# Storing the four tail tiles of the output with one DMA per batch instead of one DMA per two batches

## The chip, the cores and the metric

The kernel runs on one core of one Trainium2 chip. The metric is the device time of one execution in microseconds (us). Three runs of the kernel before gave 993.57, 993.82 and 994.36 us, a median of 993.82 us.

## What is computed

Three layers follow each other, all in 32-bit floats. The last one is the one that the change touches: its result is what is stored.

```
attention: 8 batches, 8 heads, 576 tokens, head size 64, mask by blocks of 64 tokens
x   = attention output, as 4608 tokens (8 batches x 576) x 512
soft mixture of experts, 8 experts x 4 slots:
    logits    = x @ phi                          # 4608 x 32
    slot_in   = softmax over tokens(logits).T @ x
    slot_out  = per expert: relu(slot_in @ w1) @ w2
    y         = softmax over slots(logits) @ slot_out
feed-forward:
    out = relu(y @ w_in)**2 @ w_out              # 4608 x 512, float32
```

The output has 4608 rows of 512 floats (2 KB a row). The rows of one batch stand together: batch b holds rows 576 b to 576 b + 575.

## The kernel before

The 4608 tokens are handled as 36 tiles of 128 tokens. A batch has 576 tokens, which is four whole tiles (NU = 4) and a tail of 64. Tiles 0 to 31 are the whole tiles of the eight batches. Tiles 32 to 35 are tail tiles: each holds the 64 tail tokens of two neighbouring batches, the first batch on partitions 0 to 63 and the second on partitions 64 to 127.

The attention and the experts come first. The last stage is `ffn()`. It works through six groups of six tiles (NG = 6), and in each group through 16 blocks of the hidden width. In every block and for every tile, three matmuls (L1289, L1290, L1291) add to that tile's accumulator `po`, which fills one PSUM bank. Hidden blocks for later steps (`hidden`, L1237) are made two steps ahead.

In the last of a group's 16 blocks each tile is finished in turn, and `emit_out` is called right behind its third matmul. It does two things:

- L1260 copies `po` into an SBUF tile `ot` of 128 partitions x 512 floats. VectorE (DVE) copies the even tiles and ScalarE (ACT) the odd ones. There are six `ot` buffers.
- A DMA on SyncE's queue (SP) stores `ot` to the output. For tiles 0 to 31 this is L1263, 128 consecutive rows of the output. For tiles 32 to 35 this is L1266: the output is viewed as batches x tokens x width, and the DMA's destination is two batches x 64 tokens x 512.

The sixth group holds tiles 30 to 35, so the four tail tiles are the last four things that the kernel computes and stores. Nothing follows but the end of the program, where SP waits for the DMAs that are still under way (line L1350 in the profile) and the engines meet. The instructions of each engine keep the order that the program has; SP issues one DMA after another and does no arithmetic.

Of the kernel before, what the change touches and what calls it, by code (L numbers as in the profile page):

```python
# [23 lines left out]
def tile_attn_soft_moe_ffn(  # L24
# [12 lines left out]
    nc = tc.nc  # L37
    B, H, S, D = q.shape
# [7 lines left out]
    NU = S // 128  # L46
# [1134 lines left out]
    def ffn():  # L1181
# [76 lines left out]
        def emit_out(i, po):  # L1258
            ot = o_p.tile([128, DM], F32, tag="ot", name="ot")
            (nc.scalar.copy if i % 2 else nc.vector.tensor_copy)(ot, po)  # L1260
            if i < NU * B:
                r0 = S * (i // NU) + 128 * (i % NU)
                nc.sync.dma_start(out=out[r0:r0 + 128, :], in_=ot)  # L1263
            else:
                b0 = 2 * (i - NU * B)
                nc.sync.dma_start(out=out.rearrange("(b s) d -> b s d", s=S)[b0:b0 + 2, 128 * NU:S, :], in_=ot)  # L1266

        seq = [(g, f) for g in range(NTILE // NG) for f in range(KF)]
        hid = {}
# [9 lines left out]
        for i, (g, f) in enumerate(seq):  # L1279
# [7 lines left out]
            for t in range(NG):  # L1287
                sl = slice(128 * t, 128 * t + 128)
                nc.tensor.matmul(pos[t], gh[:, sl], woh[f], start=(f == 0), stop=False)  # L1289
                nc.tensor.matmul(pos[t], gh[:, sl], wol[f], start=False, stop=False)  # L1290
                nc.tensor.matmul(pos[t], gl[:, sl], woh[f], start=False, stop=(f == KF - 1))  # L1291
                if f == KF - 1:
                    emit_out(NG * g + t, pos[t])
# [61 lines left out]
```

## Time and profile before

| | |
|---|---|
| median of three runs | 993.82 us (993.57 to 994.36) |
| the profiled execution: its time | 995.41 us |
| the profiled execution: its span, first to last instruction | 993.6 us |
| TensorE (PE) busy | 906.1 us, 91% of the span |
| DVE, ACT, POOL busy | 601.0, 519.7, 261.8 us |
| DMA from the core | 113.02 MB, 47.5% of 16 engines' span on SP's queue |
| stores of the output | 36 DMAs of 256 KB |

The span runs from the first to the last instruction; 1.8 us of the profiled execution's time lie around it. A median of the runs stands 1.6 us below the profiled execution. The page cuts the span into 40 slices of 24.8 us. In its last slice PE's digit is 0 while the slice before is at 9.

### The profile page before, as it was taken

The numbers are of one execution on the slowest core, as the hardware profiler recorded it, in microseconds if no ns is written. First come the engines' busy times: TensorE is split into PE (matmuls) and PEld (weight loads), VectorE is DVE, ScalarE is ACT, GpSimd is POOL, SyncE is SP. The second block draws the span as 40 slices with busy tenths as digits, with TensorE's granted clock in tenths as the row PEclk, the third lists the DMA queues.
The fourth block names the chain that finished last, engine by engine and source line by source line (L and its number), as shares of the span: only waits on it lengthen the run. The fifth ranks groups of instructions, "written<-read, shape, count | busy, mean of one in ns | idle before, by whom it ended". The sixth has DMA issues, their size and how long they took to land.

```text
span 993.6 us, 19542 instructions
## 1 busy us (share of the span) xinstructions
PE 906.1 (91%) x7712; PEld 656.4 (66%) x7712; DVE 601.0 (60%) x1348; ACT 519.7 (52%) x916; POOL 261.8 (26%) x390
## 2 busy tenths in 40 slices
PE   3799999989899989998898989999999999999990
PEld 2456656666566646666345868888888888888880
DVE  6767688887779878654525795444435445444430
ACT  5678577767677666543125766344334334334320
POOL 0446546463655546462000340000000000000000
PEclk9989999999999999998897999999999999999996
DMA  7777887978678886678995221001001001001001
GB/s 149 159 158 157 130 178 157 185 157 160 141 162 172 177 177 130 156 209 280 325 276 196 85 85 64 1 1 64 1 1 64 1 1 64 1 1 64 1 0 63
DMA packets 233508, 113.02 MB, mean 114 GB/s; under 512 B 193992, under 2 KB 210376, under 8 KB 233416
## 3 DMA queue, kind: packets, MB, share of 16 engines
q1 hardware_dynamic: 233416, 111.78, 47.5%
q8 instruction: 60, 0.98, 0.4%
q14 instruction: 32, 0.26, 0.1%
HBM read 78.71 MB, written 9.44 MB: 89 GB/s over the span
## 4 chain that ended last, share of the span: by engine, by line
PE 60%; DVE 13%; DMA 10%; ACT 5%; SPq 4%; POOL 3%; issue 2%; DVEq 0%; ACTq 0%; POOLq 0%
PE po L1289 12%; PE po L1291 12%; PE po L1290 12%; PE xm L557 4%; PE ps_h L1237 3%; PE ps_sc L484 3%; DVE pm L421 3%; DMA t<-qb 3%; PE ps_h L1075 2%; DVE dec_sq L172 1%; POOL ul L667 1%; POOL ss L527 1%; DMA s<-ka 1%; PE ps_u L658 1%; DMA ar_lo<-in_q_dram 1%
## 5 line engine op out<-in xcount | busy, mean ns | idle before, releaser
L1290 PE MATMUL po<-wol,gh 128*128 128x512 f32 x576 | 224.5, 390 | 1.3 <-POOL wol L1221 1.3
L1291 PE MATMUL po<-woh,gl 128*128 128x512 f32 x576 | 224.9, 391 | 0.0
L1289 PE MATMUL po<-woh,gh 128*128 128x512 f32 x576 | 224.7, 392 | 0.0
L1247 ACT ACTIVATE r<-ps_h 128x768 f32<-128x768 f32 (+1 forms) x97 | 77.9, 804 | 207.3 <-PE ps_h L1237 207.3
L1254 DVE TENSOR_TENSOR sq<-r 128x768 f32<-128x768 f32 x80 | 76.7, 958 | 172.5 <-ACT r L1247 172.5
L522 ACT ACTIVATE p<-ps_sc,es 128x512 f32<-128x512 f32 x192 | 130.2, 687 | 78.6 <-PE ps_sc L493 63.0
L527 POOL TENSOR_TENSOR ss<-p 128x384 f32<-128x384 f32 (+1 forms) x128 | 93.2, 748 | 152.2 <-ACT p L522 152.1
L421 DVE TENSOR_REDUCE pm<-ps_max 128x4 f32<-128x512 f32 x160 | 108.0, 683 | 31.4 <-PE ps_max L415 31.3
L1291 PEld LDWEIGHTS po<-woh,gl 128*128 128x128 f32 x576 | 108.3, 188 | 24.1
L1289 PEld LDWEIGHTS po<-woh,gh 128*128 128x128 f32 x576 | 108.2, 188 | 23.7 <-ACT woh L1220 0.2
L1290 PEld LDWEIGHTS po<-wol,gh 128*128 128x128 f32 x576 | 108.5, 188 | 21.6 <-POOL wol L1221 1.8
L527 POOL TENSOR_TENSOR ss<-ss,p 128x320 f32<-128x320 f32 (+1 forms) x128 | 102.4, 800 | 51.2 <-ACT p L522 46.2
L484 PE MATMUL ps_sc<-t,s 128*128 128x512 f16 (+3 forms) x512 | 108.0, 306 | 7.5 <-ACT t L395 3.1
L1255 DVE TENSOR_TENSOR gl<-sq,gh 128x768 fp32r<-128x768 f32 (+1 forms) x97 | 93.0, 959 | 16.7 <-ACT sq L1252 6.7
L557 PE MATMUL xm<-p,ar_hi 128*64 128x256 f32 (+3 forms) x512 | 93.0, 455 | 0.0
L1248 ACT ACTIVATE gh<-r 128x768 fp32r<-128x768 f32 (+1 forms) x97 | 81.6, 841 | 2.8
L407 PE MATMUL ps_max<-s,t 128*128 128x128 f16 (+3 forms) x256 | 61.9, 307 | 4.2 <-DVE pm L421 3.7
L568 PEld LDWEIGHTS tl<-p,ar_hi 128*64 128x64 f32 x512 | 36.4, 140 | 36.5 <-issue 31.8
L493 PEld LDWEIGHTS <-s 128*128 128x128 f16 x512 | 45.6, 101 | 16.9 <-issue 6.7
L493 PE MATMUL ps_sc<-t,s 128*128 128x64 f16 x512 | 54.6, 195 | 0.0
L1237 PE MATMUL ps_h<-cts,ws 128*128 128x512 f32 x192 | 50.5, 343 | 2.7 <-ACT r L1247 2.3
L395 ACT COPY t<-ps_qT 128x1024 f16<-128x1024 f16 x64 | 40.4, 637 | 10.3 <-PE ps_qT L391 9.4
(210 smaller groups left out, 1362.0 us busy)
## 6 DMA issues: line engine op xcount, KB each, us to landing
wch<-in_moe_w_dram SPq DMA_DIRECT2D x12, 1024.0 KB, 8.2
out_dram<-ot SPq DMA_DIRECT2D x36, 256.0 KB, 2.1
ar_hi<-in_v_dram SPq DMA_DIRECT2D x64, 128.0 KB, 3.2
raw<-in_moe_w_in_dram SPq DMA_DIRECT2D x16, 512.0 KB, 5.4
wch<-in_moe_w_dram SPq DMA_DIRECT2D x32, 256.0 KB, 6.0
ar_hi<-in_moe_w_dram SPq DMA_DIRECT2D x6, 1024.0 KB, 8.9
s<-s SPq DMA_DIRECT2D x32, 144.0 KB, 2.7
ar_lo<-in_k_dram SPq DMA_DIRECT2D x32, 128.0 KB, 3.2
```

What stands on the lines that cost most here:

```text
L421: nc.vector.tensor_reduce(out=o, in_=i, axis=AX.X, op=ALU.max)
L484: nc.tensor.matmul(ps[:, c0:c0 + w].rearrange("p (s c) -> p s c", c=128), kk[:, 2 * t + hp, :], qq[:, 2 * u0 + hp:8:2, :], start=(c0 == 0 ...
L493: nc.tensor.matmul(ps[:, c0:c0 + 64], kk[:, 2 * t + hp, :], qq[:, 8, h0:h0 + 64], start=(c0 == 0 and not second), stop=(second and last),)
L522: nc.scalar.activation(out=pt, in_=ps, func=AF.Exp, scale=es[:, 0:1])
L527: add = lambda o, x, y: nc.gpsimd.tensor_tensor(out=o, in0=x, in1=y, op=ALU.add)
L557: nc.tensor.matmul(box["xm"][64 * hp:64 * hp + 64, 128 * t:512], vs[:, t, hp, :], r, start=(t == 0), stop=(t == 3),)
L1237: nc.tensor.matmul(ps[:, c0:c1], ws[:, 128 * f:128 * f + 128], cts[g][:, c0:c1], start=True, stop=True)
L1248: nc.scalar.activation(out=gh[:, p], in_=r[:, p], func=AF.Square)
L1255: nc.vector.tensor_tensor(out=gl[:, p], in0=sq[:, p], in1=gh[:, p], op=ALU.subtract)
L1289: nc.tensor.matmul(pos[t], gh[:, sl], woh[f], start=(f == 0), stop=False)
L1290: nc.tensor.matmul(pos[t], gh[:, sl], wol[f], start=False, stop=False)
L1291: nc.tensor.matmul(pos[t], gl[:, sl], woh[f], start=False, stop=(f == KF - 1))
```

## The change

A tail tile is stored by two DMAs in place of one. Each takes 64 partitions of `ot` and writes 64 consecutive rows of the output, the tail of one batch. The bytes and the places they go to are the same.

```
             else:
                 b0 = 2 * (i - NU * B)
-                nc.sync.dma_start(out=out.rearrange("(b s) d -> b s d", s=S)[b0:b0 + 2, 128 * NU:S, :], in_=ot)
+                for h in range(2):
+                    r0 = S * (b0 + h) + 128 * NU
+                    nc.sync.dma_start(out=out[r0:r0 + 64, :], in_=ot[64 * h:64 * h + 64, :])
```

In the program of before, the end of SP's instructions reads as follows: the stores of tiles 30 and 31 and then those of tiles 32 to 35. The number behind `ot` tells the tiles apart. In brackets are the semaphores that a row waits for, those of DMAs (DMAHW0 to DMAHW7, taken in turn) and of the engine that made the copy.

```order
L1263 DMA out_0_dram<-ot_11719 128x512 [waits DMAHW2_49,DVE_49]
L1263 DMA out_0_dram<-ot_11725 128x512 [waits DMAHW3_49,Activation_49]
L1266 DMA out_0_dram<-ot_11731 2x64x512 [waits DMAHW4_49,DVE_49]
L1266 DMA out_0_dram<-ot_11737 2x64x512 [waits DMAHW5_49,Activation_49]
L1266 DMA out_0_dram<-ot_11743 2x64x512 [waits DMAHW6_49,DVE_49]
L1266 DMA out_0_dram<-ot_11749 2x64x512 [waits DMAHW7_49,Activation_49]
L1350 UNCONDITIONAL_BRANCH
```

Tile 35 is the row of `ot_11749`, the last DMA of the program. In the changed program the same place on SP reads so:

```order
L1263 DMA out_0_dram<-ot_11719 128x512 [waits DMAHW2_49,DVE_49]
L1263 DMA out_0_dram<-ot_11725 128x512 [waits DMAHW3_49,Activation_49]
L1268 DMA out_0_dram<-ot_11731 64x512 [waits DMAHW4_49,DVE_49]
L1268 DMA out_0_dram<-ot_11731 64x512 [waits DMAHW5_49]
L1268 DMA out_0_dram<-ot_11738 64x512 [waits DMAHW6_49,Activation_49]
L1268 DMA out_0_dram<-ot_11738 64x512 [waits DMAHW7_49]
L1268 DMA out_0_dram<-ot_11745 64x512 [waits DMAHW0_49,DVE_49]
L1268 DMA out_0_dram<-ot_11745 64x512 [waits DMAHW1_49]
L1268 DMA out_0_dram<-ot_11752 64x512 [waits DMAHW2_49,Activation_49]
L1268 DMA out_0_dram<-ot_11752 64x512 [waits DMAHW3_49]
L1352 UNCONDITIONAL_BRANCH
```

Four rows became eight. The first half of a tile waits for the copy, the second half only for a DMA semaphore. By the turn of these semaphores, the last two rows (tile 35) name those that the stores of tiles 30 and 31 name too, eight places ahead. On PE, DVE, ACT and POOL no instruction is added, removed or moved; only line numbers behind the change are two higher.

## Rows read from the trace of the kernel before

**Rows 1.** The span; then busy us by stretch (instructions), granted clock, DMA share, GB/s.
```profile
core 0: 993.6 us, clock 0.967
900.00:971.00 71.00, 70.64 (x317) 58.02 (x315) 29.20 (x32) 25.23 (x32) 0.00 (x0) 1.00 0.06 21
971.00:993.60 22.60, 0.00 (x0) 0.00 (x0) 0.00 (x0) 0.26 (x1) 0.00 (x0) 0.60 0.12 46
```
**Rows 2.** Timeline of the end: start, us, engine, line, operation [idle before].
```profile
968.00 0.91 SPq L1263 DMA_DIRECT2D out_dram<-ot  x2
...
968.64 0.69 DVE L1260 COPY ot<-po 128x512 f32<-128x512 f32 x1 [0.67 <-PE po L1291]
...
969.32 0.59 ACT L1260 COPY ot<-po 128x512 f32<-128x512 f32 x1 [0.77 <-PE po L1291]
...
969.36 9.69 SPq L1266 DMA_DIRECT2D out_dram<-ot  x4
...
970.00 0.69 DVE L1260 COPY ot<-po 128x512 f32<-128x512 f32 x1 [0.67 <-PE po L1291]
...
970.68 0.58 ACT L1260 COPY ot<-po 128x512 f32<-128x512 f32 x1 [0.77 <-PE po L1291]
```
**Rows 3.** The same columns as rows 1, for stretches around the last stores.
```profile
968.80:970.20 1.40, 1.40 (x8) 1.17 (x7) 0.73 (x2) 0.59 (x1) 0.00 (x0) 1.00 0.99 367
970.60:992.20 21.60, 0.04 (x1) 0.00 (x0) 0.09 (x1) 0.58 (x1) 0.00 (x0) 0.61 0.13 48
...
992.30:992.40 0.10, 0.00 (x0) 0.00 (x0) 0.00 (x0) 0.00 (x0) 0.00 (x0) 0.50 0.06 21
992.50:992.60 0.10, 0.00 (x0) 0.00 (x0) 0.00 (x0) 0.00 (x0) 0.00 (x0) 0.50 0.00 0
```
**Rows 4.** SP's instructions at the program's end (L1350), 990 to 994 us.
```profile
L1350 SPq EVENT_SEMAPHORE  x3: 17/17/28, 992.8 to 993.5; - x3
L1350 SPq DRAIN  x3: 7/7/13, 992.8 to 993.2; - x3
```
**Rows 5.** Stores by line: ns min/median/max of the issue, first to last start.
```profile
L1263 SPq DMA_DIRECT2D out_dram<-ot x32: 332/332/1781, 611.9 to 968.6; - x32
DMA to landing us min/median/max: 2.0/2.1/4.1
L1266 SPq DMA_DIRECT2D out_dram<-ot x4: 535/2062/4732, 969.4 to 974.3; - x4
```
**Rows 6.** Stores of the last two groups; the store of 968.58; L1266 from 971.2 on.
```profile
DMA to landing us min/median/max: 2.0/2.1/2.3
out_dram<-ot SPq DMA_DIRECT2D x1, 256.0 KB, 2.2
L1266 SPq DMA_DIRECT2D out_dram<-ot x2: 3456/4094/4732, 970.8 to 974.3; - x2
```
**Rows 7.** The columns of rows 1, for the six stores of the fifth group.
```profile
898.20:902.20 4.00, 4.00 (x20) 3.30 (x19) 2.87 (x5) 2.68 (x4) 0.00 (x0) 1.00 0.97 361
902.50:902.60 0.10, 0.10 (x2) 0.07 (x1) 0.10 (x1) 0.00 (x0) 0.00 (x0) 1.00 0.53 185
```
**Rows 8.** Loads of 64 partitions, columns of rows 5.
```profile
L271 SPq DMA_DIRECT2D ar_hi<-in_v_dram x64: 476/587/1442, 19.8 to 414.4; - x64
L294 SPq DMA_DIRECT2D ar_hi<-in_k_dram x8: 621/633/640, 23.6 to 313.3; - x8
```
**Rows 9.** SP's first issues; then DMA share in tenths, slices of 0.1 us from 0.
```profile
0.73 1.46 SPq L294 DMA_DIRECT2D ar_lo<-in_k_dram  x2
2.23 1.15 SPq L287 DMA_DIRECT2D ar_lo<-in_k_dram  x2
DMA  0000000000000000000000037753002567245679
GB/s 0 0 0 0 0 0 0 0 0 0 0 0 0 0 0 0 0 0 0 0 0 0 13 87 166 156 131 85 18 10 69 133 136 169 57 102 136 151 172 230
```

## The prediction

> **What bounds the kernel now.** I read the end of the kernel first, since only the last four stores change. The stretches [rows 1] show PE busy for 70.64 of the 71 us before 971, and then a span that goes on for 22.6 us with no PE, DVE or POOL at all. The timeline [rows 2] names the last arithmetic: ACT copies tile 35 from 970.68 to 971.26 (970.68 + 0.58). From there to the end at 993.6 are 22.3 us in which only stores run. So up to 971 the kernel is bound by PE, and behind that by the four tail stores.
>
> The stretches around the stores [rows 3] say why these take so long. From 968.8 to 970.2 the stores of tiles 30 and 31, in the whole-tile form, keep the DMA engines at a share of 0.99 and move 367 GB/s. From 970.6 to 992.2 the tail stores are under way, and the share is 0.13 at 48 GB/s. Of 16 engines 0.13 is two engines (2/16 = 0.125). The sum agrees: four tiles of 262,144 bytes are 1.05 MB, and 1.05 MB at 48 GB/s are 21.8 us, which is the length of the tail. Two engines at 48 GB/s are 24 GB/s each, and 367 GB/s over 16 are 23 each: each engine works at its usual speed, there are just two of them. What differs in form between these stores and those of L1263 is the destination, whose outermost dimension is 2 and not 128. I take it that a DMA is dealt out over its outermost rows.
>
> SP shows the backlog. A whole-tile store costs it 332 ns, while L1266 reaches 4732 [rows 5], and the two later tail stores (from 970.8 and 974.3) take 3456 and 4732 [rows 6]. The last packets pass between 992.3 and 992.5 [rows 3], SP passes its wait at 992.8 [rows 4], and the meeting of the engines takes the last 0.8 us to 993.6.
>
> **The change part by part.** What goes: the four stores that use two engines. What comes: eight stores of 64 rows (128 KB each). Arithmetic is unchanged, so ACT's last copy still ends at 971.26, and the closing 0.8 us stays. The new end is: when SP issues the eighth half, plus the time until it lands, plus 0.8.
>
> Are 64 rows dealt out over more than two engines? The trace has such a DMA by itself, at the very start: SP issues the first L294 load at 0.73, 64 partitions and 64 KB, then a second, and L287 only from 2.23 [rows 9]. The packets from 2.2 to 2.9 us carry (13 + 87 + 166 + 156 + 131 + 85 + 18) GB/s x 0.1 us = 65.6 KB, so this is the first load alone, and the share reaches 0.7, or 11 engines. A DMA of 64 rows is thus not held to two.
>
> Issue cost of a half store: no row shows this form. The nearest is L1263, same direction and same 2 KB rows but twice as many, at 332 ns [rows 5]. From above, loads of 64 partitions in short pieces: L271 with a median of 587 and L294 with 633 ns [rows 8]. From below it could be half of 332, 0.17 us, if it goes with the rows. I take 0.33, the row nearest in form, and keep 0.17 and 0.64.
>
> SP's queue with 0.33: a copy is stored about 0.03 us after it ends (968.64 + 0.69 = 969.33, issue at 969.36 [rows 2]). Copies of tiles 32 to 35 end at 969.33, 969.91, 970.69 and 971.26. The halves go out at 969.36 and 969.69 (tile 32), 970.03 and 970.36 (33), 970.72 and 971.05 (34), 971.39 and 971.72 (35). SP just keeps up with the copies: the pairs cost 0.66 and the copies come 0.64 apart, so the extra issues are hidden behind PE except the one of the last half, 0.33 us, and a little lag.
>
> Landing: whole-tile stores land 2.0 to 2.3 us after issue [rows 6], the 2.3 in a backlog of six. A half has half the data, so this is if anything high. With 2.2: 971.72 + 2.2 + 0.8 = 974.7.
>
> Is the rate then the limit? The fifth group's six whole stores moved at 361 GB/s from 898.2 on and were done by 902.6 [rows 7]. Six tiles are 1.57 MB, 4.4 us at that rate; from 968.8 that gives 973.2, plus the 0.45 us from the last packet to SP's wait (992.35 to 992.8) and 0.8: 974.4. The two limits nearly coincide, and the issue ends last.
>
> Added waits: the last half names the DMA semaphore of tile 31's store, eight places ahead. That store was issued at 968.58 (968.00 + 0.91 less its own 0.33) and took 2.2 us [rows 6], so it is in at 970.8, before 971.72: nothing. If it took the longest of the 32, 4.1 us [rows 5], SP would stand until 972.7 and the end would be 1.0 us later. Nothing stands behind it on SP but the final wait. No other engine waits for these stores, since no `ot` buffer is used again.
>
> A rule of the Trainium skill speaks against the change: DMA: Bandwidth & Descriptors, section Rules for kernel authors, advises against two transfers to disjoint partition halves, as both spread over the same 16 engines, and wants one 128-partition transfer. By it there would be nothing to win and the additional issues to pay. The share of 0.13 [rows 3] takes away its ground here: the one transfer does not use 16 engines.
>
> Sum: the span goes from 993.6 to 974.7, 18.9 us less. Against the profiled execution's 995.41 that is 976.5; against the median of the runs, 993.82, which stands 1.6 us lower, it is **974.9 us**. With 0.17 us an issue and a landing shortened by half a tile's data (0.36 us at 361 GB/s), the eighth half goes at 971.29 + 0.17 = 971.46 and lands 1.7 later: span 974.0, time 974.2.
>
> **The rivals.**
>
> *SP becomes the bound.* If a half costs 0.64 us, as L294, SP falls behind: the eighth goes at 969.36 + 7 x 0.64 = 973.84, lands by 976.1, span 976.9, time 977.1. For it: all DMAs of 64 partitions in the trace cost over 0.47 us. Against it: those read many short pieces, while the store of long rows costs 332 ns.
>
> *Half the rate.* A DMA that reads only 64 of the 128 partitions might move at half of 361 GB/s. 1.05 MB at 180 GB/s are 5.8 us from 970.2, so data ends at 976.0; plus 0.45 and 0.8, span 977.3, time 977.5. For it: L294 reached only 0.7, at 166 GB/s. Against it: its pieces are short, and halves of both kinds are in the queue at once. The Trainium skill (DMA: Bandwidth & Descriptors, section Why a DMA increments its semaphore by 16 and not by 1) lets a DMA use the largest number up to 16 that divides the slowest dimension of both sides; this would be 2 before and 16 after, and nothing there halves the rate.
>
> *The stores stay on two engines.* If the two are tied to this place or to the output's tail rows and not to the shape, 1.05 MB still takes its 21.8 us: span 993.6, time 993.8. Against it: L1263 writes the same tensor from the same buffers with all 16.
>
> *Slower: the long issue is a price per tail store.* If the 4.73 us of the last L1266 belong to each instruction and not to the backlog, eight in a row start at 969.36 and the eighth at 969.36 + 7 x 4.73 = 1002.5; with 2.3 and 0.8 the span is 1005.6, time 1005.8. It decides from about 3.0 us an issue on ((993.6 - 0.8 - 2.3 - 969.4) / 7). Against it: the shortest L1266 took 535 ns and only the last two took more than 3 us, when the two engines had a backlog.
>
> **How the numbers follow.** The forecast has 0.66, the SP bound 0.18, half the rate 0.09, no change 0.04, slower 0.03. A measurement of this kernel can tell about 0.2%, 2 us, from no change; the first three are far beyond this, so faster has 0.93, same 0.04, slower 0.03. The range reaches from 973.8 (the low end of 974.2 less the 0.4 by which runs differ) to 977.6, which takes in the SP bound and half the rate; it leaves out some 0.1.
>
> **What would show it.** In the profile after, the stretch from the last copy to the end should be near 3.4 us and not 22.3; the DMA share there near 1 until about 973; eight issues on SP, each near 0.33 us, with none over 1; the last of them starting near 971.7. Issues near 0.6 with a share well under 1 would mean the SP bound, short issues with a share near 0.5 half the rate. A share of 0.13 with 48 GB/s would prove the reading of the outermost dimension wrong. PE's end before 970.7 should not move.

## The result and the profile after

The changed kernel took a median of 979.51 us in four runs (976.15 to 982.93), the kernel before 993.70 us in the four beside them (993.56 to 994.36). The ratio is 0.9856 with a 95% interval of 0.9816 to 0.9896. So it is faster, by 14 us or 1.4%. The forecast was 974.9 with a range of 973.8 to 977.6: the direction was right and the median lies 1.9 us above the range.

The profiled execution of the changed kernel is one of those four runs, 977.51 us with a span of 975.7. The timeline of its end (columns of [rows 2]) shows where the old tail went:

```profile
967.10 0.69 DVE L1260 COPY ot<-po 128x512 f32<-128x512 f32 x1 [0.67 <-PE po L1293]
...
967.78 0.59 ACT L1260 COPY ot<-po 128x512 f32<-128x512 f32 x1 [0.77 <-PE po L1293]
967.82 5.00 SPq L1268 DMA_DIRECT2D out_dram<-ot  x8
...
968.72 0.39 PE L1293 MATMUL po<-woh,gl 128*128 128x512 f32 x1
969.14 0.59 ACT L1260 COPY ot<-po 128x512 f32<-128x512 f32 x1 [0.77 <-PE po L1293]
```

PE's last matmul ends at 969.11 and ACT's last copy at 969.73. From that copy to the end of the span are 6.0 us (975.72 - 969.73), where [rows 2] gave 22.3. The forecast was 3.4. The eight issues take SP 5.00 us, where the forecast had some 2.7. The stretches (stretch, its length, busy us by engine, granted clock, DMA share, GB/s) answer to [rows 3]:

```profile
967.30:968.60 1.30, 1.30 (x7) 1.07 (x7) 0.63 (x2) 0.59 (x1) 0.00 (x0) 1.00 1.03 383
969.00:974.00 5.00, 0.11 (x1) 0.00 (x0) 0.16 (x1) 0.59 (x1) 0.00 (x0) 0.78 0.93 207
```

The first is the two whole tiles, the second the half stores. The share rose from 0.13 to 0.93, so all 16 engines work. But they move 207 GB/s and not 383, and are busy all the same. Per busy engine that is 207 / (0.93 x 16) = 13.9 GB/s against 383 / 16.5 = 23.2: each engine needs 1.7 times as long for the same 2 KB rows. The store lines (columns of [rows 5]) show the second surprise:

```profile
L1263 SPq DMA_DIRECT2D out_dram<-ot x32: 332/333/1953, 610.4 to 967.0; - x32
L1268 SPq DMA_DIRECT2D out_dram<-ot x8: 532/564/593, 967.8 to 972.2; - x8
```

A store of 64 rows costs SP 564 ns, more than one of 128 rows. With the small gaps, the halves follow each other every 0.63 us (from 967.8 to 972.2 in seven steps). Behind them the closing part is longer than before too: the last packets pass by 974.3, and SP's last steps are these:

```profile
L1352 SPq EVENT_SEMAPHORE  x7: 17/28/28, 974.6 to 975.7; - x7
L1352 SPq DRAIN  x3: 7/7/7, 975.0 to 975.3; - x3
```

From SP's first drain to the end it is 0.76 us, as in [rows 4] (0.8). But all the waits ahead of it (974.6 to 975.0, some 0.3 us) now come after the last data, where before all but one of them had passed by 987.7, while the two engines were still writing.

PE's last matmul in the kernel before is this one:

```profile
970.25 0.39 PE L1291 MATMUL po<-woh,gl 128*128 128x512 f32 x1
```

Of the 17.9 us by which the span is shorter, 16.35 lie behind PE's last matmul (22.97 us before, 970.64 to 993.61; 6.62 after) and 1.53 before it (970.64 against 969.11). The second part is not the change's: PE's program is the same, and three runs below move this time by 2 to 5 us without any edit.

### The profile page after: what moved, and what is told of

It is laid out like the page before. It is cut to its first block, busy times and chain, and to the rows that moved or that the text cites. A ratio compares the mean times of both kernels' runs of the same rounds, so it can differ in the third digit from the quotient of the medians.

```text
span 975.7 us, 19546 instructions
## 1 busy us (share of the span) xinstructions
PE 906.2 (93%) x7712; PEld 656.4 (67%) x7712; DVE 600.3 (62%) x1348; ACT 519.3 (53%) x916; POOL 262.6 (27%) x390
## 4 chain that ended last, share of the span: by engine, by line
PE 59%; DVE 14%; DMA 11%; ACT 6%; POOL 4%; SPq 4%; issue 3%; DVEq 0%; ACTq 0%
PE po L1291 12%; PE po L1293 12%; PE po L1292 12%; PE xm L557 3%; PE ps_h L1237 3%; DMA raw<-in_moe_w_in_dram 3%; PE ps_sc L484 3%; DVE pm L421 2%; DMA s<-ka 2%; DMA t<-qb 2%; POOL ul L667 2%; POOL ss L527 2%; PE ps_h L1075 2%; DVE dec_sq L172 2%; DVE ka L375 1%
```

## The experiments

Two questions were open. Why is the end 6.0 us and not 3.4? And why do four runs of the changed kernel lie 6.8 us apart, when those of before lay within 0.8? Twelve runs followed, each with a trace. The number that the stores decide is the time from PE's last matmul to the end of the span: 22.97 us before, 6.62 in the changed kernel.

**The changed kernel again.** No edit.

> The changed kernel as it is, to see whether its scatter (976.15 to 982.93 us) belongs to it. Theory S1: the time up to PE's last matmul swings by some us in any build, since stretches at the granted clock 0.5 fall differently before 550 us; then the runs of the kernel before scatter in this call too, by 2 us or more. Theory S2: only the changed program swings; then the kernel before stays within 1 us (993.5 to 994.4) and this one scatters from 976 to 983 again. By both, the stretch from the last copy to the end of the span is 6.0 us and the 64-row stores move at 205 GB/s.

Median 976.22 us (972.23 to 983.30, six runs). The kernel before, in eleven runs on the same chip, went from 988.45 to 996.74, median 993.14. So S2 falls: the kernel before scatters as well, and its first four runs merely lay close. The ratio is 0.9843 (0.9805 to 0.9881). The end is as in the first trace, 6.60 us from PE's last matmul.

**All tiles in the whole form.**

```
-            if i < NU * B: ...
-            else: ...
+            r0 = 128 * i
+            nc.sync.dma_start(out=out[r0:r0 + 128, :], in_=ot)
```

> All 36 tiles are stored in the whole-tile form, tile i to rows 128 i to 128 i + 127, so the output's rows are permuted. Bytes and number of stores are those of the kernel before. Theory T (the tail is set by the form of the last stores): share near 0.99 and 360 GB/s to the end, issue 0.33 us, and 3.2 to 3.6 us from the last copy to the end of the span, 2.6 us less than the changed kernel. If instead the end of the program costs 6 us whatever the stores are, it is 6.0 here too. By S1 its median scatters like the changed kernel's; by S2 it stays within 1 us.

Median 975.98 (971.60 to 977.27), ratio 0.9819 (0.9789 to 0.9850). From the last copy to the end 3.02 us, from PE's last matmul 3.65. Theory T holds: the end of the program is not 6 us whatever is stored. Note that 3.0 is what the forecast's way of reckoning gives for stores that do issue at 332 ns and move at full rate, which the stretch shows (columns as above; the second row is PE's last matmul):

```profile
964.50:968.50 4.00, 1.72 (x8) 1.10 (x6) 1.10 (x2) 1.18 (x2) 0.00 (x0) 1.00 1.02 379
965.83 0.39 PE L1287 MATMUL po<-woh,gl 128*128 128x512 f32 x1
```

Its runs scatter by 5.7 us, as S1 has it.

**Half stores from every second partition.**

```
-                    nc.sync.dma_start(out=out[r0:r0 + 64, :], in_=ot[64 * h:64 * h + 64, :])
+                    nc.sync.dma_start(out=out[r0:r0 + 64, :], in_=ot[h::2, :])
```

> As the changed kernel, but a 64-row store takes every second partition of the tile (0, 2, 4, ... or 1, 3, 5, ...) and not 64 neighbours, so the tail tokens land in other rows. Theory T1 (64 neighbouring partitions supply only half the rate): here the rate is above 300 GB/s and the time from the last copy to the end 4 to 4.7 us, set by eight issues of 0.56 us. Theory T2 (a store of 64 rows is slow by its row count, four to an engine): 205 GB/s and 6.0 us as in the changed kernel.

One run, 978.76 us. The stretch and the store line (columns as above):

```profile
970.60:975.40 4.80, 0.03 (x1) 0.00 (x0) 0.08 (x1) 0.58 (x1) 0.00 (x0) 0.88 0.58 215
L1268 SPq DMA_DIRECT2D out_dram<-ot x8: 544/567/587, 969.3 to 973.8; - x8
```

The rate of 215 GB/s looks like T2, but the share beside it is 0.58, not 0.93. Per busy engine it is 215 / (0.58 x 16) = 23.2 GB/s, the speed of whole-tile stores. So T1 is right about the partitions: 64 neighbours are slow, 64 spread ones are not. The end is hardly nearer, though: 5.73 us from the last copy, 0.26 less than in the changed kernel. The engines now stand idle between the halves, because SP still needs 0.63 us for each. My expectation of 4 to 4.7 us had not multiplied the issue out.

**Two queues.** The second half of each tile is issued by ACT (lines shortened).

```
-                    nc.sync.dma_start(out=out[r0:r0 + 64, :], ...
+                    (nc.scalar if h else nc.sync).dma_start(out=out[r0:r0 + 64, :], ...
```

> As the changed kernel, but the second half of each tail tile (partitions 64 to 127) is issued on ACT's queue, so both halves of a tile are under way at the same time. Theory T1 (each half of the partitions has its own limit of about 205 GB/s): together they move at 330 to 400 GB/s, and the time from the last copy to the end is 3.5 to 4.2 us. Theory T2 (64-row stores are slow in themselves on all 16 engines): 205 GB/s in sum and 6.0 us. Rival on the issue alone: the rate does not rise, but the last issue starts 0.6 us earlier; 5.4 us.

Median 975.43 (971.18 to 979.04), ratio 0.9830 (0.9794 to 0.9866). The end is 3.92 us from the last copy, as T1 had it, but the copy itself is late; from PE's last matmul it is 5.38. The rate reaches 324 GB/s in a stretch of 1 us, a little under T1's 330, and is 271 over the whole tail. The two stretches, and the timeline of the end:

```profile
965.20:966.20 1.00, 0.00 (x0) 0.00 (x0) 0.00 (x0) 0.59 (x1) 0.00 (x0) 1.00 0.91 324
964.40:968.20 3.80, 0.09 (x1) 0.00 (x0) 0.14 (x1) 0.59 (x1) 0.00 (x0) 0.88 0.87 271
```

```profile
963.20 3.24 SPq L1268 DMA_DIRECT2D out_dram<-ot  x4
963.21 2.12 ACTq L1268 DMA_DIRECT2D out_dram<-ot  x3
...
964.10 0.39 PE L1293 MATMUL po<-woh,gl 128*128 128x512 f32 x1
965.37 0.59 ACT L1260 COPY ot<-po 128x512 f32<-128x512 f32 x1 [1.61 <-DVE ot L1260]
```

ACT copies tile 35 only at 965.37, 0.88 us after PE has finished it (964.49), because three issues stand before the copy in ACT's order.

**Two queues, the same half.** The edit, set against the run with two queues (lines shortened):

```
-  ...in_=ot[64 * h:64 * h + 64, :])
+  ...in_=ot[0:64, :])
```

> As the run with two queues, but ACT's queue stores partitions 0 to 63 a second time in place of 64 to 127, so the odd batches' tails hold wrong rows. Eight issues on two queues as there, and both DMAs of a tile draw on the same half of the partitions. Theory T1 (64 neighbouring partitions supply some 205 GB/s in all): 200 to 215 GB/s until the end, packets of 150 ns and more, 5.4 to 6.2 us from the last copy to the end. Theory T3 (the halves were slow only through SP's issue cadence of 0.63 us): as with two queues, bursts near 390 GB/s and 3.9 us.

One run, 978.04 us. With twice the issuing, the rate stays where it was:

```profile
969.50:974.50 5.00, 0.00 (x0) 0.00 (x0) 0.04 (x1) 0.59 (x1) 0.00 (x0) 0.73 0.97 202
```

A share of 0.97 at 202 GB/s, to the end: T1 holds and T3 falls. From PE's last matmul it takes 6.76 us, from the last copy 4.94; the latter missed the expected 5.4 because here too the copy is late behind ACT's issues. Together with the run before, this is the limit by itself: 64 neighbouring partitions supply some 205 GB/s, both halves at once more (324 GB/s in one stretch of the two-queue run).

**Two queues, every second partition.** Both limits taken away: the second half of a tile is issued on ACT's queue, and each half is `ot[h::2, :]`.

> As the run with two queues, but each half takes every second partition (rows land elsewhere). If SP's issue and the limit of 64 neighbouring partitions are the only two costs, packets stay near 86 ns and the end is at least as near to PE's last matmul as with two queues (5.4 us), about 5.0; ACT's last copy is still late behind its three issues. If a third cost holds it, it stays at 5.4 or more with fast packets.

One run, 971.94 us. The end is 4.89 us from PE's last matmul, 3.41 from the last copy; while data flow:

```profile
965.20:966.90 1.70, 0.04 (x1) 0.00 (x0) 0.09 (x1) 0.58 (x1) 0.00 (x0) 1.00 1.03 377
```

377 GB/s with halves of 64 rows. No third cost is needed; what stays above the whole-tile run's 3.65 is mostly ACT's late copy (it ends 1.48 us behind PE's last matmul, against 0.62 in the whole-tile run).

**Issue by shape.** The whole tiles of four groups are stored in pieces (shortened; a comment stands for the stores behind its condition).

```
+                if i // NG == 1:   # two of 64 rows
+                elif i // NG == 2: # four of 32 rows
+                elif i // NG == 3: # 96 rows and 32 rows
+                elif i // NG == 4: # two of 128 rows x 256
```

> The changed kernel, whose whole tiles are stored in other shapes by group: second group two of 64 rows, third four of 32, fourth one of 96 and one of 32, fifth two of 128 rows and half the width; all bytes as before. It measures the issue on SP by shape with nothing else under way. Theory I1 (issue cost goes by the partitions: 128 are cheap, fewer are dear): 128 x 256 at 0.33 to 0.37 us, 64, 96 and 32 rows at 0.5 to 0.6. Theory I2 (it goes by the position, 0.33 for each first store of a tile and more for a second one behind it): the second column half is dear too, and a first half of 64 rows cheap. The tail is the changed kernel's, 6.0 us.

One run, 974.22 us. The issues on SP in ns (min/median/max), in the order 64, 32, 96 and the 32 behind it, 128 x 256, 128 x 512:

```profile
L1265 SPq DMA_DIRECT2D out_dram<-ot x12: 536/593/1338, 678.8 to 686.6; - x12
L1268 SPq DMA_DIRECT2D out_dram<-ot x24: 362/425/691, 750.2 to 761.2; - x24
L1270 SPq DMA_DIRECT2D out_dram<-ot x6: 317/369/373, 821.5 to 827.7; - x6
L1271 SPq DMA_DIRECT2D out_dram<-ot x6: 423/432/1975, 821.9 to 828.2; - x6
L1274 SPq DMA_DIRECT2D out_dram<-ot x12: 350/414/452, 892.9 to 898.2; - x12
L1276 SPq DMA_DIRECT2D out_dram<-ot x8: 332/332/443, 607.4 to 964.1; - x8
```

Both theories fail. The cost does not go by the partitions: 64 rows are the dearest at 593, dearer than 32 (425) and 96 (369). It does not go by the place in the tile alone either: a tile's first half of 64 rows took 536 to 548 ns, save one of 1338, and its second 591 to 602, so the place is worth some 50 ns, but no first half comes near 0.33 us. Why just 64 rows cost more stays open. What is shown is that the price hangs on the shape and that, by the medians, fewer rows than 128 are not cheaper. The tail took 5.7 us from the last copy, where 6.0 were expected.

**Tail tiles earlier, with the store of before.** The last stage's groups run in another order, so that the four tail tiles are stored while PE works on four more groups.

```
-        seq = [(g, f) for g in range(NTILE // NG) for f in range(KF)]
+        seq = [(g, f) for g in (0, 5, 1, 2, 3, 4) for f in range(KF)]
```

> The store of before (one DMA for two batches), but the groups of the last stage run in the order 0, 5, 1, 2, 3, 4: the tail tiles come second and the last six tiles are whole. Theory T (the end is set by the form of the last stores alone, and the long tail stores cost nothing where PE works beside them): the two-engine stores take their 22 us inside the next group, PE does not wait, and from the last copy to the end of the span it is 3.0 us as in the run with whole rows only, 19.3 us less than before; ratio to before near 0.980. Rival: the stores hold SP and `ot` buffers up, and PE or the copies of the next group wait; then some us come back.

Median 975.28 (972.02 to 976.57), ratio to before 0.9784 (0.9743 to 0.9826), with eleven runs of before between 990.76 and 1002.42 around them. The two-engine stores are still there, and cost nothing:

```profile
L1266 SPq DMA_DIRECT2D out_dram<-ot x4: 535/2012/4732, 683.7 to 688.6; - x4
687.00:705.00 18.00, 18.00 (x83) 14.85 (x81) 7.90 (x9) 6.76 (x9) 0.00 (x0) 1.00 0.13 50
L1263 SPq DMA_DIRECT2D out_dram<-ot x32: 332/333/1902, 610.9 to 970.2; - x32
```

The share is 0.13 at 50 GB/s (0.13 at 48 in [rows 3]), and PE is busy for all of the 18 us. From the first store of the output (610.9) to the end of PE's last matmul (969.58) it is 358.7 us, as in the kernel before (611.9 in [rows 5] to 970.64). So PE waited for nothing, and the rival falls. It also settles that the two engines come with the store and not with the place at the end of the program. The end is 3.66 us from PE's last matmul.

**Both changes together.** The half stores in that order.

> The changed kernel's store and the order of groups 0, 5, 1, 2, 3, 4 together. By theory T the form of the tail stores no longer matters: 3.0 us from the last copy to the end, the same time as the store of before in this order, and 3.0 us less than the changed kernel. If the halves themselves cost PE something (contention), this one is slower than the other.

Median 973.52 (972.39 to 978.36), ratio 0.9788 (0.9748 to 0.9828), the same as with the store of before. Hidden behind PE, the form of the tail stores makes no difference clear of the noise. The end was 3.94 us from PE's last matmul in its trace.

**Changed kernel and new order side by side.** Two kernels already known, on one chip.

> The changed kernel beside the order 0, 5, 1, 2, 3, 4 with the store of before, on one chip. Traces so far: 6.6 us from PE's last matmul to the end here, 3.7 there. Theory S1: medians of both scatter by several us with the granted clock, so a difference of 2.9 us shows only roughly; in each run a longer span goes with a lower mean clock.

> The order 0, 5, 1, 2, 3, 4 with the store of before, once more: 2.9 us below the changed kernel's median, give or take the 3 us by which medians have moved; 3.7 us from PE's last matmul to the end.

Changed kernel: median 974.55 (973.31 to 981.10), ratio 0.9820 (0.9782 to 0.9857). New order with the store of before: 972.24 (968.94 to 973.05), ratio 0.9778 (0.9741 to 0.9814). The slowest run of the new order is below the fastest of the changed kernel. The medians differ by 2.3 us, the two ends by 2.96 (6.62 and 3.66). The two ratios of the new order with the store of before, 0.9784 and 0.9778, are the lowest here, with 0.9788 for both changes together next to them. Within the changed kernel's six runs the span goes with the mean granted clock: 971.5 us at 0.979, 972.3 at 0.978 and 0.977, 973.2 at 0.976, 975.7 at 0.974, 979.3 at 0.967.

**The kernel before once more.**

> The kernel before, for a second trace of it. Theory S1: its PE ends its last matmul at another time than 970.64 us, by up to some us, and the difference lies before 550 us, where the granted clock falls to 0.5 at other places; from there on the two traces run alike, and the end takes 22.97 us again. Theory S2: PE ends at 970.6 within 0.5 us.

One run, 997.54 us, 2.1 above the first profiled execution (995.41). PE's last matmul ends at 972.79 and not 970.64, and the end behind it is 22.95 us again. The whole-tile stores (L1263) of this trace, and below them those of the second trace of the changed kernel:

```profile
L1263 SPq DMA_DIRECT2D out_dram<-ot x32: 332/333/1283, 614.1 to 970.7; - x32
```

```profile
L1263 SPq DMA_DIRECT2D out_dram<-ot x32: 332/333/1658, 605.1 to 961.8; - x32
```

From the first to the last of them it is 356.6 and 356.7 us, as in [rows 5] (611.9 to 968.6). The first one, however, stands at 614.1, 605.1 and 611.9. In all fourteen traces it is 358.7 us from the start of the first store to the end of PE's last matmul. So all that swings lies before the first store; these lines do not show the 550 us of the expectation. One such place, first in [rows 1]'s execution, then in this one (stretch, busy us, granted clock, DMA share, GB/s):

```profile
207.00:221.50 14.50, 12.78 (x166) 9.14 (x166) 12.46 (x33) 9.09 (x19) 10.37 (x21) 1.00 0.84 161
```

```profile
207.00:221.50 14.50, 13.56 (x81) 9.02 (x81) 7.96 (x27) 7.14 (x13) 7.69 (x17) 0.53 0.53 118
```

In the second, the granted clock is at its lower level (1.2 GHz) nearly throughout, and PE gets through 81 matmuls where the other, at the upper level, did 166. The 7 us ahead of it, in the same order, had PE busy for 6.83 and 5.88 us:

```profile
200.00:207.00 7.00, 6.83 (x96) 5.24 (x95) 5.97 (x11) 4.88 (x11) 4.91 (x8) 1.00 0.87 185
```

```profile
200.00:207.00 7.00, 5.88 (x88) 4.72 (x84) 5.13 (x10) 3.42 (x9) 4.93 (x8) 1.00 0.81 172
```

S1 holds in this: the same program loses time at the lower clock in other places from run to run. That the clock is the only source is not shown. The mean clock does not order every set of runs: of the six of the changed kernel again, one has a span of 979.8 us at 0.976 and another 974.4 at 0.972. What decides where the clock falls was not found either.

## Why the prediction was right and wrong

**What bounds the end: right.** The old tail was four stores on two engines. With 64 rows outermost the share rises to 0.93, and in the new order the old form still runs at 0.13 in another place. The rival of stores that stay on two engines is refuted; so is the rival of a long issue as a price per store (the longest half store took 593 ns).

**Issue cost of a half store: wrong, and the main term that was mis-sized.** I took 0.33 us from the whole-tile store as the row nearest in form. It is 0.56, and 0.63 from one half to the next, within the bound from the loads of 64 partitions (0.64). The nearest row had the same direction and row length, but these did not set the price; the loads of 64 partitions were nearer, though the runs leave open why. The sum had the eighth half go out 0.46 us behind the last copy (971.72 - 971.26); it went out 2.5 us behind it. That is 2.05 of the 2.55 us by which the end came out longer; the rest is a later landing and the longer closing part. Every second partition shows the term alone: fast packets, and still 5.73 us from the last copy, against the 3.44 forecast. In the low end of the forecast the landing is out by 0.1 us (2.2 - 0.36 is 1.84 and not 1.7), which decides nothing.

**The rate: wrong.** I reckoned with 361 GB/s; the halves move at 207. This was the second rival, with 0.09, and its price, a span end 6.0 us behind the last copy (977.3 - 971.26), is what was measured. That it fits so closely is in part luck: the data ended 0.2 us sooner behind the copy than it had reckoned, and the closing part took 0.2 us longer. My reason against this rival, that halves of both kinds are in the queue at once, did not help on one queue: there they moved at the 202 to 207 GB/s of one half alone, and only on two queues did they reach 324. The sign that I had named, a share near 0.5, was wrong too: all 16 engines were busy, at a share of 0.93, and each was slow. Issue and rate give almost the same pace: a half is issued every 0.63 us, and 131 KB at 207 GB/s take 0.63 us. So each was enough by itself, and taking away one of them alone won 0.27 us (every second partition, 6.35 us from PE's last matmul) or nothing (two queues on the same half, 6.76, against 6.62). I priced the two rivals apart and gave them 0.27; what happened was both at once, with the end of the slower of them. The Trainium skill's rule on the number of engines (DMA: Bandwidth & Descriptors, section Why a DMA increments its semaphore by 16 and not by 1) held: the share was 0.13, two engines, before and 0.93 after.

**The Trainium skill's advice against transfers to disjoint partition halves** (DMA: Bandwidth & Descriptors, section Rules for kernel authors), which I had set aside: half right here. That the two serialize holds for one queue (207 GB/s) and not for two (324 GB/s, where one half alone had 202). The halves won 16.35 us over a store on two engines, since that had been held back by its shape, but they lose 2.97 us from PE's last matmul to a whole-tile store (6.62 and 3.65).

**ACT's last copy stays at 971.26: wrong, and the reason that the median left the range.** The end measured in the trace gives 16.35 us less, so 993.7 - 16.35 = 977.35, inside the range and 2.45 us above the forecast: that much is the issue and the rate. The other 2.2 us to 979.51 are put down to the part before the change. Only one of the four runs has a trace, but in all three traces of the changed kernel the end takes 6.60 to 6.62 us. I had read the spread of that part off three runs within 0.8 us and allowed 0.4. The traces have PE's last matmul anywhere from 963.8 to 972.8 us with the same instructions on PE up to the last stage. Sixteen runs of the changed kernel have a median of 976.2 us, inside the range, and go from 972.2 to 983.3. Its three medians, 979.51, 976.22 and 974.55, lie 5 us apart, so by my estimate a range for one of them had to be some 3 us wider to each side.

**Added waits: right.** The last half was issued in step with the others; no issue took over 0.6 us.

**Sign: right.** All ratios to before lie between 0.978 and 0.986.

## What to carry to other kernels

Look at the DMA share of the last stores: 0.13 at an unchanged speed per engine means two engines, and a small outermost dimension in the destination is the first thing to look at. Splitting such a store costs issues and may run at half speed, so first try to finish those tiles earlier, where 22 us of slow storing cost nothing; that one-line order beat the split and needed no other store. And before a range is drawn from a handful of close runs, look whether the granted clock falls inside the body: runs of the changed kernel, where it does, lay up to 11 us apart.

## What the runs showed of the hardware that was not expected

- Stores from 64 neighbouring partitions moved at 202 to 207 GB/s with all 16 engines busy; those from every second partition ran each engine at the speed of whole-tile stores (215 GB/s at a share of 0.58), and on two queues reached 377.
- SP's issue of a 512-float-wide store took 332 ns for 128 rows, 369 for 96, 425 for 32 and 564 to 593 for 64.
- DMA issues on ACT's queue stood in the way of ACT's own work: three issues of 2.12 us together put off the last copy by 0.85 us.
